# Cross-attention, Fourier mixing and FFN on one core: the Fourier stage on folded data, attention with block-diagonal state, u kept on chip, the row scale behind the second matmul

## The chip, the cores and the metric

One core of one Trainium2 chip. The metric is device time in microseconds. The engines of a core take their instructions in the order of their own list and wait on semaphores: PE (matrix multiply, with PEld loading its weights), DVE (vector), ACT (scalar functions), POOL and SP, both of which also issue DMAs.

## The reference

Eight batches. Attention runs in both directions between x (8 heads, 512 rows, 64 wide) and a small state (32 rows a head); the results are joined to 544 rows of 512, mixed by the real part of a two-dimensional Fourier transform, normalised by row, and sent through an FFN of 512 to 2048 to 512.

```
scores = scale * np.matmul(x, state.transpose(0, 1, 3, 2))      # 512 x 32 per head
xread  = softmax(scores) @ state
sread  = softmax(scale * np.matmul(state, x.transpose(0, 1, 3, 2))) @ x
x      = heads side by side of [xread, sread]                     # 8 x 544 x 512
u      = x + np.real(fft(fft(x, axis=1), axis=2))
un     = (u - mean) / np.sqrt(var + 1e-06)                        # by row
out    = u + np.maximum(un @ w_ch1, 0.0) @ w_ch2
```

(softmax is written out in the reference, and the joining is shortened here.)

## The kernel before

First the tables of cosines and sines are computed (L21, on DVE and ACT: CN, SNneg for the columns, CM, SM for the rows), and both weights are loaded on POOL's queue (L100, L101). Then `fft_attention(b)` for the eight batches, then `ffn(t)` for 34 tiles of 128 rows. A scheduler turns this program into one list per engine, so that FFN tiles of early batches stand between the attention steps of later ones; what depends on what is enforced by semaphores, and pools of buffers (psA with tags qa and qb, psF with ph and po, all in PSUM) limit how far a stage runs ahead.

`fft_attention(b)` loads x and state (L112, L114) and takes two heads at a time (the loop at L126). For each pair: x is transposed (L131, xTp to xT), the scores of x against the state are one matmul per head and 128 rows, 32 columns wide (L138, psc); exp, row sums, and eight scalings on DVE (L148, a); eight transposes back (L152); xread by matmuls that fill half the partitions (L160). The other direction makes scores 32 x 512 (L168), exp (L172), scale (L174), transposes (L178), and then the result twice, once in each orientation: srp (L189) and srTp (L191) alternate, 64 and 32 columns each.

The Fourier stage multiplies the transposed rows by CN and SNneg (L206, L208, 288 of the 512 columns, the rest by mirroring at L213 and L214), and then by CM and SM over the five row chunks: for each of five tiles of output rows, ten matmuls of 512 columns (L222, L225, pMix). x itself is transposed back (L231) and added (L234, u). u is written to DRAM (L237); mean and variance (L240, L241), the square root on ACT (L243), the reciprocal, the scaled row un (L248), and its transpose (L252, unTp) go to unT_all on chip.

`ffn(t)` takes 128 rows: 64 matmuls of 128 columns (L268, ph_p), ReLU on ACT (L270, hT), 16 matmuls of 512 columns (L273, po); u is read back from DRAM (L276), added (L278, ot), and stored (L279).

## Time and profile before

| | us |
|---|---|
| median of 3 runs (lowest, highest) | 682.48 (681.53, 682.55) |
| the profiled execution: span from first to last instruction | 674.9 |
| PE busy / DVE busy / ACT busy | 598.5 / 319.3 / 273.3 |
| first matmul of attention (L117) waits for | 48.2 |
| last matmul of the FFN (L273) ends, last ot (L278) begins | 671.05 |

The profile follows one execution. For this execution it gives its span; the times of the runs are a little longer than the span, since they include what lies around it. Line numbers are those of the listing. In the lists of groups, "out<-in" names the tiles, then partitions x elements and type, the count, the busy time in us, the mean duration of one in ns, and behind the last bar the idle time ahead of the group and what ended it. In the chain and in the timeline the first two numbers are the start and the duration in us. A row of a stretch gives, after its bounds, the length, and then for PE, PEld, DVE, ACT and POOL the busy time and the count of instructions, then the granted clock, the share of DMA and GB/s. Matmuls are pipelined: the duration of one is longer than the step from its start to the next one's.

### The profile page before, as it was taken

To read this page: it belongs to the slowest core of one execution; us is meant where nothing else is said; L and a number is where in the kernel's file an instruction comes from. 1 tells how busy PE (TensorE), PEld (TensorE's weight loads), DVE (VectorE), ACT (ScalarE), POOL (GpSimd) and SP (SyncE) were. 2 spreads that over 40 slices of the span, in tenths; PEclk is the share of its full clock that TensorE was granted. 3 is DMA by queue.
4 is the path that set the end of the run, shared out by engine and by line. 5 is a ranking of instruction groups with operands and counts; after the bars stand their busy time and mean duration, and the time that the engine had idled before them with its cause. 6 is when DMAs were issued, how large, how long until landed. Compare 5 with 4: busy or idle time off the path is not lost. (4 is left out here: it accounts for less than half of the span.)

```text
span 674.9 us, 13333 instructions
## 1 busy us (share of the span) xinstructions
PE 598.5 (89%) x5648; PEld 376.1 (56%) x5648; DVE 319.3 (47%) x962; ACT 273.3 (40%) x601; POOL 39.3 (6%) x60
## 2 busy tenths in 40 slices
PE   0006689999999999999999999999999999999997
PEld 0003455665566746665566566655655566567775
DVE  8934334644554556445644654464436543611010
ACT  2212224633453436353634453355335533433322
POOL 2040010001000100010001100110000000000000
PEclk9999999999989999899999999998989898999999
DMA  7691052105211512151215211521102000222221
GB/s 138 112 59 8 0 34 83 65 17 50 79 52 34 50 63 66 35 48 49 80 35 35 80 51 32 50 84 33 32 9 90 33 33 1 98 63 82 77 64 48
DMA packets 52507, 36.24 MB, mean 54 GB/s; under 512 B 36832, under 2 KB 38880, under 8 KB 52448
## 3 DMA queue, kind: packets, MB, share of 16 engines
q0 software_dynamic: 37664, 8.65, 13.9%
q1 hardware_dynamic: 14784, 26.75, 11.8%
q8 instruction: 44, 0.72, 0.4%
q14 instruction: 15, 0.12, 0.1%
HBM read 26.21 MB, written 17.83 MB: 65 GB/s over the span
## 5 line engine op out<-in xcount | busy, mean ns | idle before, releaser
L268 PE MATMUL ph_p<-unT_all,w 128*128 128x128 bf16 x2176 | 148.5, 220 | 2.9 <-ACT hT L270 2.9
L273 PE MATMUL po<-w,hT 128*128 128x512 bf16 x544 | 144.8, 388 | 2.2 <-ACT hT L270 1.7
L268 PEld LDWEIGHTS <-w 128*128 128x128 bf16 x2176 | 126.5, 98 | 18.0 <-issue 6.1
L270 ACT ACTIVATE hT<-ph_p 128x512 bf16<-128x512 f32 x136 | 80.2, 598 | 87.6 <-PE ph_p L268 87.1
L273 PEld LDWEIGHTS <-hT 128*128 128x128 bf16 x544 | 46.4, 99 | 45.8 <-issue 4.5
L278 DVE TENSOR_TENSOR ot<-po,ut 128x512 f32<-128x512 f32 x34 | 23.4, 689 | 76.6 <-PE po L273 76.2
L133 DVE COPY xT<-xTp 64x1024 bf16<-64x1024 bf16 x32 | 21.8, 682 | 79.5 <-PE xTp L131 79.5
L189 PE MATMUL srp<-xin,a2T 128*32 128x64 bf16 x256 | 52.3, 207 | 1.5 <-DVE a2T L181 1.5
L191 PE MATMUL srTp<-a2T,xin 128*64 128x32 bf16 x256 | 52.4, 207 | 0.0
L222 PE MATMUL pMix<-A,CM 128*128 128x512 bf16 (+1 forms) x200 | 49.8, 379 | 2.1 <-DVE A L213 1.4
L225 PE MATMUL pMix<-Bm,SM 128*128 128x512 bf16 (+1 forms) x200 | 51.1, 379 | 0.0
L172 ACT ACTIVATE e<-p 32x512 f32<-32x512 f32 x64 | 37.3, 583 | 33.2 <-PE p L168 33.0
L234 DVE TENSOR_TENSOR u<-pMix,xbt 128x512 f32<-128x512 f32 x32 | 22.1, 691 | 55.7 <-ACT xbt L233 33.3
L117 PE MATMUL stTp<-ident,st 32*64 32x32 bf16 x64 | 3.5, 184 | 48.2 <-POOL xbS L124 48.2
L206 PE MATMUL pA<-CN,xbT 128*128 128x288 bf16 (+1 forms) x160 | 44.9, 311 | 0.0
L208 PE MATMUL pB<-SNneg,xbT 128*128 128x288 bf16 (+1 forms) x160 | 44.5, 310 | 0.0
L152 PE MATMUL aTp<-ident,a 128*32 128x128 bf16 x256 | 37.6, 234 | 7.1 <-DVE a L148 6.0
L210 DVE CAST A<-pA 128x288 bf16<-128x288 f32 (+1 forms) x40 | 18.2, 455 | 50.5 <-PE pA L206 50.5
L148 DVE TENSOR_SCALAR a<-e,ssum 128x32 bf16<-128x32 f32 x256 | 40.9, 234 | 0.9
L193 ACT CAST xbS<-srp 32x128 bf16<-32x128 f32 x32 | 8.2, 255 | 73.4 <-PE srp L189 73.4
L254 ACT COPY unT_all<-unTp 128x512 bf16<-128x512 bf16 (+1 forms) x40 | 20.4, 518 | 42.0 <-PE unTp L252 42.0
L152 PEld LDWEIGHTS <-a 128*32 128x32 bf16 x256 | 17.4, 98 | 34.1 <-DVE a L148 24.7
(81 smaller groups left out, 711.4 us busy)
## 6 DMA issues: line engine op xcount, KB each, us to landing
ut<-u_dram SPq DMA_DIRECT2D x34, 256.0 KB, 2.8
out_dram<-ot SPq DMA_DIRECT2D x34, 256.0 KB, 2.0
u_dram<-u SPq DMA_DIRECT2D x32, 256.0 KB, 2.0
w<-in_moe_w_ch_dram POOLq DMA_DIRECT2D x2, 2048.0 KB, 17.8
xin<-in_x_dram POOLq DMA_DIRECT2D x8, 512.0 KB, 7.0
u_dram<-u SPq DMA_DIRECT2D x8, 64.0 KB, 1.8
st<-in_state_dram POOLq DMA_DIRECT2D x8, 32.0 KB, 2.2
```

The costliest lines, as they stand in the source:

```text
L148: nc.vector.tensor_scalar_mul(a[:, hl, si, :], e[:, hl, si, :], ssum[:, hl, si, :])
L152: nc.tensor.transpose(aTp[:, hl, si, :], a[:, hl, si, :], ident)
L172: nc.scalar.activation(e2, p2, AF.Exp, scale=scale, accum_out=ssum2)
L189: nc.tensor.matmul(srp[:, hl, :], lhsT=a2T[:, hl, si, :], rhs=xhsi, start=(si == 0), stop=(si == SC - 1))
L191: nc.tensor.matmul(srTp[hl * 64:hl * 64 + 64, :], lhsT=xhsi, rhs=a2T[:, hl, si, :], start=(si == 0), stop=(si == SC - 1))
L206: nc.tensor.matmul(pA[:m_sz, :], lhsT=xbT[:, c, sl], rhs=CN[:, c, :], start=(c == 0), stop=(c == DC - 1))
L208: nc.tensor.matmul(pB[:m_sz, :], lhsT=xbT[:, c, sl], rhs=SNneg[:, c, :], start=(c == 0), stop=(c == DC - 1))
L222: nc.tensor.matmul(pMix[:m_sz, :], lhsT=CM[:, c, msl], rhs=A[:, c, :], start=(c == 0), stop=False)
L225: nc.tensor.matmul(pMix[:m_sz, :], lhsT=SM[:, c, msl], rhs=Bm[:, c, :], start=False, stop=(c == MC - 1))
L268: nc.tensor.matmul(ph_p[:, mcl, :], lhsT=w1[:, kc, mc * 128:(mc + 1) * 128], rhs=unT[:, kc, :], start=(kc == 0), stop=(kc == DC - 1))
L270: nc.scalar.activation(hT[:, half * MCPH:(half + 1) * MCPH, :], ph_p, AF.Relu)
L273: nc.tensor.matmul(po, lhsT=hT[:, kc, :], rhs=w2[:, kc, :], start=(kc == 0), stop=(kc == FC - 1))
```

## The change

The real part of the transform is the same at (row s, column n) and at (row -s, column -n). The new kernel uses this twice. Each batch's rows are put down as XF (rows 1 to 256) and XR (the mirrored rows 543 to 288, with their columns mirrored); Sm is their sum, and XE and XO are its even and odd parts over the columns, 256 wide (XN holds the middle column). One product with the row tables (gep, gop, 288 output rows, tables CT, ST, CL, SL) and one with the column table T2 (yp) serves both a row and its mirror: U is yp + XF and yp + XR. The 32 rows left (0 and 257 to 287) of four batches are collected in XL and GL, and make one tile of 128 for the FFN (`front_low`).

Attention takes four heads at once. The state stands block-diagonally in stb (four heads of 32 rows on 128 partitions, with columns of ones, so that a matmul gives the row sums too). xT is 128 partitions high; exp is taken on 128 x 1024 (ET in one orientation, E in the other); xread comes out in the needed row order, forwards or reversed, and DVE divides by the sums when it moves it out of PSUM (L278). The state's reads come as srp (257 columns) and are put into XR by eight small operations (L295).

u stays in SBUF. Rows are centred but not scaled before the transposes (ub, L349); since ReLU passes a positive factor, the scale of the row is applied behind the second matmul (L405: po times rstd, plus u). rstd is a power of -0.5 on POOL (L203) in place of the square root on ACT. The FFN takes the 512 rows of a batch at once (ph of 512 columns), with one ReLU in four on DVE (L396). Mirrored rows come out in reversed order: they go to DRAM (r_dram, L412), and from there reversed to the output (L413). x is loaded in five pieces (L74), two batches ahead; the weights in six (L84, L87), on POOL's queue ahead of the tables' iotas. psQ has two buffers of two banks for all of a front's products, psF two each for ph and po.

The new program is `front(b)`, then `ffn` of the batch before it. The removed lines are those of the listing above; these are added (cut to the core):

```diff
+    r_dram = nc.dram_tensor("r_dram", (B, 2, 128, dm), F32, kind="Internal")
+    def load_x(b):
...
+        for ps, si, rows in (
+            (slice(0, 128), 0, xb[1:129]),
+            (slice(0, 128), 1, xb[129:257]),
+            (slice(0, 1), 2, xb[0:1]),
+            (slice(1, 128), 2, xb[257:384]),
+            (slice(0, 128), 3, xb[384:512]),
+        ):
+            nc.gpsimd.dma_start(out=t[ps, si, 1:513].rearrange("p (h d) -> p h d", d=D), in_=rows)
+    load_x(0)
+    for q in range(4):
+        nc.gpsimd.dma_start(out=w1[:, :, q * 512:(q + 1) * 512], in_=w1v[:, :, q * 512:(q + 1) * 512])
+    load_x(1)
+    for q in range(2):
+        nc.gpsimd.dma_start(out=w2[:, q * 8:(q + 1) * 8, :], in_=w2v[:, q * 8:(q + 1) * 8, :])
...
+                nc.vector.tensor_scalar(f[:, i, :], in0=lf, scalar1=pf[:, c:c + 1], scalar2=None, op0=ALU.mult)
+            nc.vector.tensor_scalar(q, in0=f, scalar1=1.0 / N, scalar2=float(1 << 23), op0=ALU.mult, op1=ALU.add)
+            nc.vector.tensor_scalar(q, in0=q, scalar1=float(1 << 23), scalar2=-float(N), op0=ALU.subtract, op1=ALU.mult)
+            nc.vector.tensor_add(f, f, q)
+            nc.vector.tensor_scalar(q, in0=f, scalar1=-1.0, scalar2=None, op0=ALU.mult)
+            nc.vector.tensor_max(q, q, f)
...
+    psQ = ctx.enter_context(tc.tile_pool(name="psQ", bufs=2, space=bass.MemoryType.PSUM))
+    psF = ctx.enter_context(tc.tile_pool(name="psF", bufs=2, space=bass.MemoryType.PSUM))
...
+    def stats_of(u, name):
+        st6 = wk.tile([128, 6], F32, name="st6", tag="st6", bufs=4)
+        nc.vector.bn_stats(st6, u)
+        mv = wk.tile([128, 2], F32, name="mv", tag="mv", bufs=6)
+        nc.vector.bn_aggr(mv, st6)
+        nc.gpsimd.tensor_tensor(rstd, mv[:, 1:2], epst, op=ALU.add)
+        nc.gpsimd.tensor_tensor(rstd, rstd, mhalf, op=ALU.pow)
+        return mv, rstd
...
+    def front(b):
...
+            nc.tensor.transpose(sTp[:, 0, pr * 128:(pr + 1) * 128], sb[:, g, 4 + 128 * hp:132 + 128 * hp], ident)
+        sT = wk.tile([128, 4, 128], BF16, name="sT", tag="sT")
+        nc.vector.tensor_copy(sT, sTp[:, 0, 0:512].rearrange("p (a b) -> p a b", b=128))
...
+            for si in range(4):
+                o = (pr % 2) * 512 + si * 128
+                nc.tensor.transpose(xTp[:, g, o:o + 128], xin[:, si, 1 + 128 * pr:129 + 128 * pr], ident)
+        nc.vector.tensor_copy(xT[:, 0:2, :], xTp[:, 0, :].rearrange("p (a b) -> p a b", b=S))
+        nc.scalar.copy(xT[:, 2:4, :], xTp[:, 1, :].rearrange("p (a b) -> p a b", b=S))
...
+        for g in range(2):
+            for lo, hi, src in ((0, NM, slice(0, NM)), (NM, S, slice(S - 1, NM - 1, -1))):
+                for hp in range(2):
+                    nc.tensor.matmul(eTp[:, g, lo:hi], lhsT=sT[:, 2 * g + hp, :], rhs=xT[:, 2 * g + hp, src],
+                                     start=(hp == 0), stop=(hp == 1))
+        ET = wk.tile([128, 2, S], BF16, name="ET", tag="ET")
+        nc.scalar.activation(ET, eTp, AF.Exp, scale=scale)
...
+        for si in range(4):
+            for pr in range(4):
+                hp = pr % 2
+                nc.tensor.matmul(
+                    esp[:, si // 2, o:o + 64].rearrange("p (h j) -> p h j", j=Ns),
+                    lhsT=xT[:, pr, si * 128:(si + 1) * 128],
+                    rhs=sT[:, pr, 64 * hp:64 * hp + 64].rearrange("p (h j) -> p h j", j=Ns)[:, :, ::-1],
+                    start=True, stop=True)
+        nc.scalar.activation(E.rearrange("p a b c -> p (a b c)"), esp.rearrange("p a b -> p (a b)"), AF.Exp, scale=scale)
...
+        for g in range(2):
+            for si in range(4):
+                nc.tensor.matmul(srp[:, g, 0:257], lhsT=E[:, si, g, :], rhs=xin[:, si, 257 * g:257 * g + 257],
+                                 start=(si == 0), stop=(si == 3))
+        rcs = wk.tile([128, 2], F32, name="rcs", tag="rcs")
+        nc.vector.reciprocal(rcs, srp.rearrange("p g c -> p (g c)")[:, 0:769:768])
...
+        def xread(c0, rev, name):
+            p = q2(name)
+            for half in range(2):
+                g = 1 - half if rev else half
+                rhs = sb[:, g, 259::-1] if rev else sb[:, g, 4:264]
+                nc.tensor.matmul(p[:, half, 0:260], lhsT=ET[:, g, c0:c0 + 128], rhs=rhs, start=True, stop=True)
+            return p
...
+            rs = wk.tile([128, 2, 4], F32, name="rs", tag="rs", bufs=4)
+            nc.vector.reciprocal(rs[ps], p[ps, :, 256:260])
+            nc.vector.tensor_tensor(
+                o.rearrange("p (g h d) -> p g h d", g=2, d=D),
+                in0=p[ps, :, 0:256].rearrange("p g (h d) -> p g h d", d=D),
+                in1=rs[ps].unsqueeze(3).to_broadcast([n, 2, 4, D]),
+                op=ALU.mult,
...
+        for k in range(2):
+            p = xread(128 * k, False, "xfp")
+            normalise(p, XF[:, k, 0:512])
+            p = xread(256 + 128 * k, True, "xrp")
+            normalise(p, XR[:, k, 1:513])
+            if k == 0:
+                for g in range(2):
+                    for hh in range(4):
+                        c0 = 512 - (256 * g + 64 * hh)
+                        ph = slice(32 * hh, 32 * hh + 32)
+                        nc.vector.tensor_scalar(
+                            XR[0:32, 0, c0:c0 - 64:-1], in0=srp[ph, g, 1 - g + 64 * hh:65 - g + 64 * hh],
+                            scalar1=rcs[ph, g:g + 1], scalar2=None, op0=ALU.mult)
+        p = xread(256 - 32 * bq, False, "xlp")
+        normalise(p, XL[pq, 0:512], pq)
+        Sm = wk.tile([128, 2, 514], BF16, name="Sm", tag="Sm")
+        nc.vector.tensor_add(Sm, XF, XR)
+        nc.vector.tensor_add(XE[:, 0:2, :], Sm[:, :, 0:256], Sm[:, :, 512:256:-1])
+        nc.vector.tensor_sub(XO[:, 0:2, 1:256], Sm[:, :, 1:256], Sm[:, :, 511:256:-1])
+        nc.gpsimd.tensor_copy(XN[:, 0:2, 0:1], Sm[:, :, 256:257])
+        nc.vector.tensor_add(XE[pq, 2, :], XL[pq, 0:256], XL[pq, 512:256:-1])
+        nc.vector.tensor_sub(XO[pq, 2, 1:256], XL[pq, 1:256], XL[pq, 511:256:-1])
+        nc.gpsimd.tensor_copy(XN[pq, 2, 0:1], XL[pq, 256:257])
...
+        for j in range(2):
+            for c in range(3):
+                nc.tensor.matmul(gp[:, j, 0:NM], lhsT=XE[:, c, 128 * j:128 * j + 128], rhs=cos[c],
+                                 start=(c == 0), stop=(c == 2))
+        nc.scalar.copy(G[:, 0:2, :], gp[:, :, 0:NM])
...
+            for c in range(3):
+                nc.tensor.matmul(gp[:, j, 0:NM], lhsT=XO[:, c, 128 * j:128 * j + 128], rhs=sin[c],
+                                 start=(c == 0), stop=(j == 1 and c == 2))
+            if j == 0:
+                for c in range(3):
+                    nc.tensor.matmul(gp[:, 0, 0:NM], lhsT=XN[:, c, :], rhs=cos[c], start=False, stop=(c == 2))
+        nc.scalar.copy(G[:, 2:4, :], gp[:, :, 0:NM])
+        nc.gpsimd.tensor_copy(GLs[g4][:, :, 32 * bq:32 * bq + 32], G[:, :, 256:NM])
...
+        for k in range(2):
+            yp = q2("yp")
+            for c in range(4):
+                nc.tensor.matmul(yp[:, 0, :], lhsT=G[:, c, 128 * k:128 * k + 128], rhs=T2[:, c, :],
+                                 start=(c == 0), stop=(c == 3))
+            nc.vector.tensor_add(U[:, k, 0, 0:512], yp[:, 0, :], XF[:, k, 0:512])
+            nc.vector.tensor_add(U[:, k, 1, 1:512], yp[:, 0, 1:512], XR[:, k, 1:512])
+            nc.vector.tensor_add(U[:, k, 1, 512:513], yp[:, 0, 0:1], XR[:, k, 512:513])
+            for r in range(2):
+                u = U[:, k, r, r:r + 512]
+                mv, rstd = stats_of(u, "rstd")
+                rstds.append((k, r, rstd))
+                ub = wk.tile([128, 512], BF16, name="ub", tag="ub", bufs=4)
+                ud = u if r == 0 else U[:, k, 1, 512:0:-1]
+                nc.vector.tensor_scalar(ub, in0=ud, scalar1=mv[:, 0:1], scalar2=None, op0=ALU.subtract)
+                tp = q2("tp", BF16)
+                for j in range(DC):
+                    nc.tensor.transpose(tp[:, 0, 128 * j:128 * j + 128], ub[:, 128 * j:128 * j + 128], ident)
+                col = (2 * (1 - r) + k) * 128
+                nc.scalar.copy(unT[:, :, col:col + 128], tp[:, 0, 0:512].rearrange("p (a b) -> p a b", b=128))
...
+    def front_low(g4):
+        yp = q2("yp")
+        for c in range(4):
+            nc.tensor.matmul(yp[:, 0, :], lhsT=GLs[g4][:, c, :], rhs=T2[:, c, :], start=(c == 0), stop=(c == 3))
+        U = wk.tile([128, 512], F32, name="UL", tag="UL")
+        nc.vector.tensor_add(U, yp[:, 0, :], XLs[g4][:, 0:512])
...
+        hT = wk.tile([128, FC, 512], BF16, name="hT", tag="hT")
+        for f in range(FC):
+            ph = psF.tile([128, 512], F32, name="ph", tag="ph")
+            for c in range(DC):
+                nc.tensor.matmul(ph[:, :n], lhsT=w1[:, c, f * 128:(f + 1) * 128], rhs=unT[:, c, :],
+                                 start=(c == 0), stop=(c == DC - 1))
+            if f % 4 == 3:
+                nc.vector.tensor_scalar_max(hT[:, f, :n], ph[:, :n], 0.0)
+            else:
+                nc.scalar.activation(hT[:, f, :n], ph[:, :n], AF.Relu)
+        for i, (u, rstd, dst) in enumerate(tiles):
+            po = psF.tile([128, dm], F32, name="po", tag="po")
+            for f in range(FC):
+                nc.tensor.matmul(po, lhsT=hT[:, f, i * 128:(i + 1) * 128], rhs=w2[:, f, :],
+                                 start=(f == 0), stop=(f == FC - 1))
+            ot = wk.tile([128, dm], F32, name="ot", tag="ot", bufs=3)
+            nc.vector.scalar_tensor_tensor(ot, in0=po, scalar=rstd, in1=u, op0=ALU.mult, op1=ALU.add)
...
+                nc.sync.dma_start(out=r_dram[b, k], in_=ot)
+                nc.sync.dma_start(
+                    out=out[b, top:top - 128:-1, :].rearrange("r (c n) -> c r n", c=2),
+                    in_=r_dram[b, k].rearrange("r (c n) -> c r n", c=2))
...
+    ready = [front(0)]
+    for b in range(B):
+        if b + 1 < B:
+            if b + 2 < B:
+                load_x(b + 2) if b + 2 >= 2 else None
+            ready.append(front(b + 1))
+        ffn(*ready[b])
+        if b % 4 == 3:
+            ffn(*front_low(b // 4))
```

Where the instructions now stand. On ACT before, in the midst of the span, ReLUs of the FFN (hT) stand between the steps of one head pair's attention (e is an exp, xbT and xbS are copies of attention's results):

```order
L162 CAST xbT<-xrTp 128x512
L193 CAST xbS<-srp 32x128
L194 CAST xbT<-srTp 128x32
L141 ACTIVATE e<-psc 128x256
L270 ACTIVATE hT<-ph_p 128x512
L172 ACTIVATE e_1189,ssum_1190<-p_1187 32x512
L172 ACTIVATE e_1196,ssum_1197<-p_1194 32x512
L270 ACTIVATE hT<-ph_p 128x512
L162 CAST xbT<-xrTp 128x512
L270 ACTIVATE hT<-ph_p 128x512
```

On ACT of the new kernel, fronts 1 to 4 have eight ReLUs between E and the two copies of G; front 1 is this:

```order
L230 COPY xT<-xTp 128x1024
L398 ACTIVATE hT<-ph 128x512
L240 ACTIVATE ET<-eTp 128x1024
L254 ACTIVATE E<-esp 128x1024
L398 ACTIVATE hT<-ph 128x512 x8
L319 CAST G<-gep 128x576
L328 CAST G<-gop 128x576
L398 ACTIVATE hT<-ph 128x512 x3
L354 COPY unT<-tp 128x4x128 x4
```

and further on, behind the low tile's twelve ReLUs, fronts 5 and 6 are these:

```order
L230 COPY xT<-xTp 128x1024
L240 ACTIVATE ET<-eTp 128x1024
L254 ACTIVATE E<-esp 128x1024
L319 CAST G<-gep 128x576
L328 CAST G<-gop 128x576
L354 COPY unT<-tp 128x4x128 x4
L230 COPY xT<-xTp 128x1024
L240 ACTIVATE ET<-eTp 128x1024
L254 ACTIVATE E<-esp 128x1024
L319 CAST G<-gep 128x576
L328 CAST G<-gop 128x576
L398 ACTIVATE hT<-ph 128x512 x12
```

In fronts 5 and 6 no ReLU stands between xT and G: what FFN work there is comes behind.

On POOL before, at the program's start, ident and the iotas of the tables come first, and the loads of the weights and of x behind them:

```order
masks.py:197 MEMSET ident 128x128
L27 ISA
L27 IOTA l_i 128x288
masks.py:199 AFFINE_SELECT ident<-ident 128x128
L36 IOTA p_i 128x288
L27 IOTA l_i 128x544
L36 IOTA p_i 128x544
L100 DMA w_221<-in_moe_w_ch_dram 128x4x2048
L101 DMA w_222<-in_moe_w_ch_dram 128x16x512
L112 DMA xin<-in_x_dram 128x32x64
```

and in the new kernel:

```order
L84 DMA w_69<-in_moe_w_ch_dram 128x4x512
L74 DMA xin_60<-in_x_dram 128x8x64 x2
L74 DMA xin_60<-in_x_dram 1x8x64
L74 DMA xin_60<-in_x_dram 127x8x64
L74 DMA xin_60<-in_x_dram 128x8x64
L84 DMA w_69<-in_moe_w_ch_dram 128x4x512 x3
L74 DMA xin_61<-in_x_dram 128x8x64 x2
L74 DMA xin_61<-in_x_dram 1x8x64
L74 DMA xin_61<-in_x_dram 127x8x64
L74 DMA xin_61<-in_x_dram 128x8x64
L87 DMA w_70<-in_moe_w_ch_dram 128x8x512 x2
masks.py:197 MEMSET ident 128x128
```

Here sixteen issues (x2 and x3 are repeated rows) stand ahead of ident, and the iotas follow it.

More of the change, by code (lines that the diff above doesn't have):

```diff
@@ L71 @@
     Ns = state.shape[2]
[L72 removed]
+    dm = H * D
     Stot = S + Ns
@@ new lines @@
+    stf = singles.tile([128, B, 2, D], F32, name="stf")
+    nc.sync.dma_start(
+        out=stf.rearrange("p b g d -> p (b g) d"),
+        in_=state.rearrange("b (g hh) j d -> (hh j) (b g) d", hh=4),
+    )
+    xin_bufs = []
+    for i in range(2):
+        t = singles.tile([128, 4, 514], BF16, name=f"xin{i}")
+        xin_bufs.append(t)
+    def load_x(b):
+        t = xin_bufs[b % 2]
+        xb = x[b].rearrange("h s d -> s h d")
+        for ps, si, rows in (
[6 more added lines that the diff above has]
+            nc.gpsimd.dma_start(out=t[ps, si, 1:513].rearrange("p (h d) -> p h d", d=D), in_=rows)
```

375 lines of the change are left out of this document (156 added, 219 removed).

## The prediction

> **What bounds the kernel now.** I read the page's first two parts, then three stretches of the span, then the chain that ended last and the waits.
>
> ```profile
> span 674.9 us, 13333 instructions
> PE 598.5 (89%) x5648; PEld 376.1 (56%) x5648; DVE 319.3 (47%) x962; ACT 273.3 (40%) x601; POOL 39.3 (6%) x60
> PE   0006689999999999999999999999999999999997
> 48.60:97.50 48.90, 34.93 (x257) 21.70 (x256) 19.43 (x70) 13.15 (x36) 2.78 (x4) 1.00 0.24 16
> 120.00:590.00 470.00, 461.39 (x4311) 283.69 (x4309) 242.14 (x760) 211.94 (x481) 22.38 (x31) 0.98 0.22 49
> 597.19:671.00 73.81, 73.81 (x816) 52.83 (x814) 6.92 (x10) 24.49 (x41) 0.00 (x0) 1.00 0.20 66
> PE stTp L117 <- POOL xbS L124: 48.2, 1, 48.2
> ```
>
> PE is the bound from 120 us on (461 of 470 us busy); the first 48.2 us it waits for the tables and the first load. Busy is not full speed, so I take the pitch (start to start) from rows in sequence: the chain's tail for the FFN, the timeline for the rest.
>
> ```profile
> 642.86 3.58 PE ph_p L268 x64
> 646.44 3.45 PE po L273 x16
> 671.05 0.69 DVE ot L278
> 300.60 0.29 PE L206 MATMUL pA<-CN,xbT 128*32 128x288 bf16 x1
> ...
> 301.21 0.29 PE L208 MATMUL pB<-SNneg,xbT 128*32 128x288 bf16 x1
> 329.69 0.20 PE L189 MATMUL srp<-xin,a2T 128*32 128x64 bf16 x1
> 329.82 0.20 PE L191 MATMUL srTp<-a2T,xin 128*64 128x32 bf16 x1
> 318.95 0.36 PE L138 MATMUL psc<-stT,xT 64*128 64x32 bf16 x8
> 319.24 0.23 PE L268 MATMUL ph_p<-unT_all,w 128*128 128x128 bf16 x1
> 93.43 0.45 PE L206 MATMUL pA<-CN,xbT 128*128 128x288 bf16 x1
> 93.67 0.45 PE L208 MATMUL pB<-SNneg,xbT 128*128 128x288 bf16 x1
> ```
>
> Pitches: 512 columns 3.45/16 = 0.216 us; 128 columns 3.58/64 = 0.056; 288 columns 0.61/5 = 0.122 (six starts, the middle ones left out); 32 columns 0.29/8 = 0.036. The pair L189/L191, of different tile shapes, costs 0.13 each for 64 and 32 columns: 512 of them take 67 us. Before 97 us everything runs at half pitch (0.24 for 288 columns), though the granted clock reads 1.00. One FFN tile takes 3.58 + 3.45 = 7.03 us; after 597.19 lie 73.81/7.03 = 10.5 tiles, so 23.5 tiles (165 us) lie between 48 and 597, and the other 384 us are attention and Fourier: **48 us a batch**.
>
> **The change, part by part.** *PE work.* A front (L206 of the new kernel: attention, folded Fourier, transposed un-scaled rows) has 36 transposes at 0.056, 16 score matmuls of 64 columns (between 0.036 and 0.056, I take 0.05), 4 of 288 and 4 of 224, 8 of 257, 10 of 260, 15 Fourier ones of 288 and 8 of 512; lengths between are interpolated (0.096, 0.109, 0.110). That is 2.0 + 0.8 + 0.5 + 0.4 + 0.9 + 1.1 + 1.8 + 1.7 = 9.2 us instead of 48. The FFN of a batch is 128 matmuls of 512 columns, 27.6 us; the two tiles of low rows cost 8.2 us each with their own transposes. Sum: 8 × 36.8 + 2 × 8.2 = **311 us**. The FFN alone hardly gains (34 × 7.03 = 239 against 235); the gain is in attention and Fourier.
>
> *The pace of one front.* Its steps depend on one another, mostly through DVE. Rows for that:
>
> ```profile
> L234 DVE TENSOR_TENSOR u<-pMix,xbt 128x512 f32<-128x512 f32 x32 | 22.1, 691 | 55.7 <-ACT xbt L233 33.3 <-issue 17.3 <-DMA ut<-u_dram 2.6
> L240 DVE BATCH_NORM_STATS2 stats<-u 128x6 f32<-128x512 f32 x32 | 22.0, 689 | 0.8
> L133 DVE COPY xT<-xTp 64x1024 bf16<-64x1024 bf16 x32 | 21.8, 682 | 79.5 <-PE xTp L131 79.5
> L148 DVE TENSOR_SCALAR a<-e,ssum 128x32 bf16<-128x32 f32 x256 | 40.9, 234 | 0.9
> L144 DVE RECIPROCAL ssum<-ssum 128x8 f32<-128x8 f32 x32 | 6.2, 195 | 0.8
> L241 DVE BATCH_NORM_AGGREGATE mv<-stats 128x2 f32<-128x6 f32 x32 | 5.6, 174 | 0.8
> L248 DVE TENSOR_SCALAR un<-u,neg_mu,rstd 128x512 bf16<-128x512 f32 x32 | 17.4, 545 | 1.0
> L46 DVE TENSOR_SCALAR q_f<-q_f 128x544 f32<-128x544 f32 x5 | 2.2, 435 | 0.0
> L48 DVE TENSOR_TENSOR f<-prod,q_f 128x544 f32<-128x544 f32 x5 | 3.6, 720 | 0.0
> L172 ACT ACTIVATE e<-p 32x512 f32<-32x512 f32 x64 | 37.3, 583 | 33.2 <-PE p L168 33.0
> L254 ACT COPY unT_all<-unTp 128x512 bf16<-128x512 bf16 x32 | 18.6, 582 | 40.9 <-PE unTp L252 40.9
> ```
>
> From the first transpose: transposes 1.1 and 0.2 until they have drained; ACT's half of xT, 1024 wide, 1.05 (between 0.58 and 1.17, twice the 512-wide row; nearer the double); eTp 1.1 with drain; exp ET 1.05, exp E 1.05; srp 1.1. Then DVE: five normalisations of 0.19 + 0.69, eight reads of srp at 0.2, Sm (1028 bf16: 0.69 if it ran at twice the f32 rate, 1.3 by L48's; I take 1.2), XE and XO 0.69 each, two of 0.43, a reciprocal: 9.6, and 1.2 for the two places where DVE waits for PE's next product. Then gop 1.0, G 0.65, the last two of yp 0.6. Sum **about 19.7 us from sTp to yp, in which PE has 7.5 us of work**; 12.2 are empty unless FFN matmuls stand between. From yp to the transposes of ub are 4.3 us more (U 1.54, statistics 1.38 + 0.35, ub 1.09), per half.
>
> DVE in all: 20 us a front and 5.5 for the batch's FFN; ACT 14. Against some 46 us a batch neither is the bound. What it removes of DMA (u out to DRAM and back) buys nothing: above, ph_p and po follow each other with nothing between.
>
> *Waits in PE's order.* I walked along the orders with these durations. In fronts 1 to 4 about 53 FFN matmuls (11.4 us) stand inside the 19.7, leaving some 4 us a front, at po behind E, at gep behind XE, and at the two tp: 16. Behind front 4, yp of the second half and the low tile wait 4.5 + 2.5, the low tile's ReLUs 1.6: 8.6. Front 5 has 8 FFN matmuls inside: 9.3, then 4.2 at its second half. Front 6 has none: 12.2. Front 7 has 8: 10.5. The rest (two tp, the second low tile, the last low ReLUs) 5. Sum **66 us**.
>
> *The start.* POOL issues 16 DMAs before it makes ident and the iotas.
>
> ```profile
> L112 POOL DMA_DIRECT2D xin<-in_x_dram x8 | 13.5, 1685 | 54.0 <-DVE CM L55 35.4 <-PE srTp L191 18.5
> L114 POOL DMA_DIRECT2D st<-in_state_dram x8 | 4.7, 584 | 227.4 <-PE xrTp L160 227.4
> L124 POOL MEMSET xbS<- 128x512 bf16 x8 | 4.2, 531 | 11.2 <-DVE u L236 11.2
> ```
>
> One issue costs 0.58 for 256 pieces and 1.69 for 4096, so 0.5 + 0.29 per thousand: 4 × 0.66 (w1), 2 × 3.7 (five for each x), 2 × 0.8 (w2) = 11.6 us. Ident, two memsets of 1152 (1.1 each) and the iotas take 5 more: 17.5 us. DVE then builds both tables, ten operations on 864 or 1024 columns and eight smaller at the rates of L46 and L48, 11.5 us: 29. Front 0 follows: 2.4 until xT is copied, 17.3 from there to yp, 4 because PE's links run at half pitch, as all of PE's work did before 97 us, 4.3 for each half, 0.6 for tp and 2.2 for the next front's transposes, which stand ahead of the first FFN matmul: 35 together, so **64 us** (bounds 58, if DVE's operations overlap, and 82, if xin is late, below).
>
> *The end.* The last ot 0.7, then eight stores on SP:
>
> ```profile
> 671.77 0.33 SPq L279 DMA_DIRECT2D out_dram<-ot  x1
> u_dram<-u SPq DMA_DIRECT2D x8, 64.0 KB, 1.8
> q1 hardware_dynamic: 14784, 26.75, 11.8%
> q0 software_dynamic: 37664, 8.65, 13.9%
> xin<-in_x_dram POOLq DMA_DIRECT2D x8, 512.0 KB, 7.0
> ```
>
> 8 × 0.33 + 1.8 + 0.7 = **5 us**. Four of them have 31 rows, which no row shows; q1 spent 0.118 × 16 × 674.9 / 26.75 = 48 engine-us a MB, so 4 × 64 KB all on one engine would last 12 us: 5 to 14. I take 5, from the 32-row store. Likewise the 127-row piece of x: spread, 7 us as xin's row; on one engine its 1016 packets last 28 (7.0 × 16/4096 each) to 41 us (q0's mean of 40 ns), and front 0 starts 5 to 18 us later. [...]
>
> The two stores and the reversed read through r_dram block SP for some 2 us each, beside 3.45 us of po; three ot buffers cover that.
>
> *Sum.* 64 + (311 − 10, done by then) + 66 + 5, + 3 while PE still runs at half pitch, + 3 for a granted clock of 0.98 in mixed work (row 120 to 590) = **442 us of span**. The span of before is 674.9, the median of its runs 682.48; the 7.6 between lie outside it: **450 us**.
>
> **Rivals.** *The waits vanish* (Sm, XE, XO fast, DVE's operations overlapping, fronts 5 to 7 covered): 0 to 40 us of 66 left, 384 to 424. For it: L148's 40.9/256 = 160 ns against 234 shows that DVE's operations overlap. Against: PE takes its instructions in the order given. 0.16.
>
> *PE falls back to half pitch.* From 48.6 to 97.5 us PE was 71% busy in small pieces and stayed at half; at 97.4, in a row of matmuls without a break, it changed, and never went back, with no wait above 1.5 us. In fronts 5 to 7 it is 38% busy, with gaps of 3 to 4 us. Falling back costs the doubled links of three chains (4 each) and about 2.5 each until it recovers: +20, 470. 0.14. [...]
>
> *The uneven DMAs go to one engine*: +5 to +18 and +9, 464 to 477. 0.13.
>
> *Slower than before*: PE never leaves half pitch, because no stretch is unbroken for long enough. Then 64 + 2 × 301 + about 20 + 5 + 7.6 = 699. Over 682 from a mean pitch of 1.8 times the full one. Against it are runs of 32 to 80 FFN matmuls (7 to 17 us) with nothing between; 0.015.
>
> **How the numbers follow.** Forecast 0.56, its own range 424 to 475; rivals as above, and 0.005 for no change. The range 412 to 492 leaves out the lower half of the first rival and the far ends of the others. A measurement tells 0.2% from no change: faster 0.98, within 0.005, slower 0.015.
>
> **What would show it.** Right: ph starts at 60 to 68 us; 0.216 us for 512 columns in po; ACT's chain ET, E, G in fronts 5 to 7 about 15 us with PE mostly empty; PE busy for about 75% of the span. Wrong: a steady PE without gaps in fronts 5 to 7, a first ph after 75, or 0.43 for 512 columns after 100 us.

## The result, and the profile after

The changed kernel takes 664.14 us (median of 4 runs, 661.32 to 664.79) against 682.0 of before: a ratio of 0.973 (0.970 to 0.976). The forecast was 450 us, its range 412 to 492. The direction came out, the size didn't: nine tenths of the expected gain is missing. The profiled execution took 664.54 us, with a span of 661.0.

The page of the kernel after, first parts, queues and groups:

```profile
span 661.0 us, 5124 instructions
...
PE 359.5 (54%) x1973; PEld 181.7 (27%) x2008; DVE 205.1 (31%) x470; ACT 130.2 (20%) x217; POOL 133.2 (20%) x170
...
PE   0000104138349907960990767237599949989970
...
PEclk9999997557859956995895788558589979999995
...
q0 software_dynamic: 159584, 8.88, 23.9%
...
L74 POOL DMA_DIRECT2D xin<-in_x_dram x40 | 79.4, 1993 | 247.2 <-issue 181.1
...
L327 PE MATMUL gop<-CT,XN 128*128 128x288 bf16 x16 | 5.3, 438 | 118.4 <-POOL XN L306 118.4
```

PE's work did shrink: 359.5 us busy in place of 598.5, much of it at half pitch (the mean granted clock is 0.829). But PE is busy for only 54% of the span: it has regular notches (the slices of 0 to 4 from the twelfth on), and the granted clock falls with them (down to 5 in the row PEclk). Before, PE was full from 120 us on, and behind the first 48.2 us it never waited for POOL (6% busy). Now POOL's busiest group is L74, the load of x, with 181.1 us of idle time ahead of it that the profile puts down to "issue", that is, to nothing else in the trace. And q0, the queue of POOL's loads, moves 159,584 packets where the kernel before moved 37,664, for about the same bytes (8.88 MB and 8.65).

The waits of the kernel after (us in total, times, the longest):

```profile
POOL xin L74 <- issue: 181.1, 16, 23.8
...
PE gop L327 <- POOL XN L306: 118.4, 6, 21.1
...
PE sTp L219 <- POOL ident masks.py:199: 79.4, 1, 79.4
```

PE waits for POOL seven times: once 79.4 us for ident, in the place of the 48.2 of before, and in six fronts about 20 us for XN, a copy that itself takes 0.2 us. POOL's timeline at the program's start and in front 1 shows what XN and ident stand behind (start, duration, group, and in brackets the idle time ahead):

```profile
2.20 2.32 POOL L74 DMA_DIRECT2D xin<-in_x_dram  x3
13.01 6.69 POOL L74 DMA_DIRECT2D xin<-in_x_dram  x1 [8.50 <-issue]
35.88 0.90 POOL L74 DMA_DIRECT2D xin<-in_x_dram  x1 [16.18 <-issue]
...
165.99 6.68 POOL L74 DMA_DIRECT2D xin<-in_x_dram  x1 [3.64 <-issue]
189.28 0.91 POOL L74 DMA_DIRECT2D xin<-in_x_dram  x1 [16.61 <-issue]
190.20 0.20 POOL L306 COPY XN<-Sm 128x2 bf16<-128x2 bf16 x1
```

The fourth issue of a load is the piece of 127 rows. It takes 6.7 us where three others together take 2.3, POOL stands still ahead of it, and behind it POOL does nothing for 16 us; only then come the fifth piece and XN. On PE, the first ph (behind front 0) starts at 153.29, and in front 1 gop waits for just that XN:

```profile
153.29 1.91 PE L393 MATMUL ph<-unT,w 128*128 128x512 bf16 x4
...
190.46 0.66 PE L327 MATMUL gop<-CT,XN 128*128 128x288 bf16 x2 [19.25 <-POOL XN L306]
190.91 0.45 PE L327 MATMUL gop<-CL,XN 128*128 128x288 bf16 x1
191.15 0.69 PE L323 MATMUL gop<-ST,XO 128*128 128x288 bf16 x2
...
635.72 5.77 PE L402 MATMUL po<-w,hT 128*128 128x512 bf16 x26
```

Behind the stall the starts lie 0.24 us apart for 288 columns (190.91 to 191.15): PE is back at half pitch, and so it is behind each of the six stalls. The view of the DMA issues (count, KB each, us to landing) sets the pieces side by side:

```profile
xin<-in_x_dram POOLq DMA_DIRECT2D x24, 128.0 KB, 4.3
...
xin<-in_x_dram POOLq DMA_DIRECT2D x8, 127.0 KB, 23.0
```

One row fewer, and the landing takes 23.0 us in place of 4.3. The packets set the piece apart too: a full piece has 128 x 8 runs of 64 numbers, 1024 packets. With 128 rows in place of the 127 (the first experiment below) q0 has 37,728 packets; the 121,856 more of this kernel are 15,232 a load, so the piece makes 16,256, which is 127 x 8 x 16. The expectations below take this for runs cut into sixteenths. The bytes say otherwise: 8.88 MB against 8.40 there, so that the further packets carry 4 bytes each, on top of the data. The sizes in the trace agree: 32,768 packets of 128 bytes, the whole runs of eight batches (64 numbers of 2 bytes), and 122,720 of 4 bytes, where the version with 128 rows has 800. Each run of the piece brings 15 packets of 4 bytes with it; what they are for, the trace does not say.

At the end the stores of SP reach far beyond PE, whose last po ends at 641.49 (the row above):

```profile
637.68 12.23 SPq L408 DMA_DIRECT2D out_dram<-ot  x10
```

The span ends 19.5 us behind PE, 11 us behind the last of these issues.

### The profile page after: what moved, and what is told of

The parts are those of the page before. It is cut to its first block, busy times and chain, and to the rows that moved or that the text cites. A ratio compares the mean times of both kernels' runs of the same rounds, so it can differ in the third digit from the quotient of the medians.

```text
span 661.0 us, 5124 instructions
## 1 busy us (share of the span) xinstructions
PE 359.5 (54%) x1973; PEld 181.7 (27%) x2008; DVE 205.1 (31%) x470; ACT 130.2 (20%) x217; POOL 133.2 (20%) x170
## 3 DMA queue, kind: packets, MB, share of 16 engines
q0 software_dynamic: 159584, 8.88, 23.9%
## 4 chain that ended last, share of the span: by engine, by line
PE 40%; issue 35%; POOL 13%; DVE 7%; ACT 2%; POOLq 0%; DVEq 0%; ACTq 0%
PE po L402 17%; PE ph L393 13%; POOL xin L74 10%; PE yp L338 3%; PE tp L352 1%; PE gop L323 1%; PE gop L327 1%; DVE XR L295 1%; DVE st L198 1%; PE eTp L237 1%; PE srp L260 1%; PE xTp L228 1%; ACT E L254 1%; DVE U L340 1%; DVE XF L278 1%
## 5 line engine op out<-in xcount | busy, mean ns | idle before, releaser
L74 POOL DMA_DIRECT2D xin<-in_x_dram x40 | 79.4, 1993 | 247.2 <-issue 181.1
L393 PE MATMUL ph<-unT,w 128*128 128x512 bf16 x496 | 125.9, 392 | 2.2 <-ACT hT L398 0.7
L402 PE MATMUL po<-w,hT 128*128 128x512 bf16 x532 | 121.8, 382 | 3.9 <-DVE ot L405 3.0
L398 ACT ACTIVATE hT<-ph 128x512 bf16<-128x512 f32 (+1 forms) x120 | 63.2, 535 | 111.7 <-PE ph L393 90.4
L393 PEld LDWEIGHTS <-w 128*128 128x128 bf16 x640 | 60.5, 102 | 61.9 <-issue 15.2
L327 PE MATMUL gop<-CT,XN 128*128 128x288 bf16 x16 | 5.3, 438 | 118.4 <-POOL XN L306 118.4
L396 DVE TENSOR_SCALAR hT<-ph 128x512 bf16<-128x512 f32 (+1 forms) x40 | 24.2, 604 | 132.6 <-PE ph L393 125.9
L219 PE MATMUL sTp<-ident,stb 128*128 128x128 bf16 x32 | 3.7, 250 | 79.9 <-POOL ident masks.py:199 79.4
L405 DVE SCALAR_TENSOR_TENSOR ot<-po,rstd,U 128x512 f32<-128x512 f32 x32 | 23.2, 746 | 38.9 <-PE po L402 38.8
L338 PE MATMUL yp<-T,G 128*128 128x512 bf16 x57 | 21.9, 485 | 2.4 <-ACT unT L354 1.1
L237 PE MATMUL eTp<-xT,sT 128*128 128x288 bf16 (+1 forms) x64 | 11.5, 310 | 20.7 <-DVE xT L229 20.4
L203 POOL TENSOR_TENSOR rstd<-rstd,mhalf 128x1 f32<-128x1 f32 x34 | 21.3, 626 | 2.7
L198 DVE BATCH_NORM_STATS2 st<-U 128x6 f32<-128x512 f32 x32 | 20.4, 681 | 0.0
```

The lines of the kernel that those rows point to most:

```text
L74: nc.gpsimd.dma_start(out=t[ps, si, 1:513].rearrange("p (h d) -> p h d", d=D), in_=rows)
L198: nc.vector.bn_stats(st6, u)
L203: nc.gpsimd.tensor_tensor(rstd, rstd, mhalf, op=ALU.pow)
L237: nc.tensor.matmul(eTp[:, g, lo:hi], lhsT=sT[:, 2 * g + hp, :], rhs=xT[:, 2 * g + hp, src], start=(hp == 0), stop=(hp == 1))
L338: nc.tensor.matmul(yp[:, 0, :], lhsT=G[:, c, 128 * k:128 * k + 128], rhs=T2[:, c, :], start=(c == 0), stop=(c == 3))
L393: nc.tensor.matmul(ph[:, :n], lhsT=w1[:, c, f * 128:(f + 1) * 128], rhs=unT[:, c, :], start=(c == 0), stop=(c == DC - 1))
```

## The experiments

Two theories stood at the outset. The first: the 127-row piece alone holds POOL, and what is queued behind it there holds PE. The rival: the five-piece load as such, or the amount of POOL work in a front, is too much. The kernel before ran beside each: 676.8 to 686.5 us beside the first four, 682.4 beside the next two, 676.8 to 684.2 beside the last four.

**Another division of the rows.** Five pieces as well, but 128 rows first and then row 0 over its first row:

```diff
-            (slice(0, 1), 2, xb[0:1]),
-            (slice(1, 128), 2, xb[257:384]),
+            (slice(0, 128), 2, xb[256:384]),
+            (slice(0, 1), 2, xb[0:1]),
```

> The third piece of x has 128 rows (256 to 383, on partitions 0 to 127) in place of 127, and row 0 is then put over partition 0; nothing else differs. Theory A (the 127-row piece is cut into very small packets, 16256 a load, which fill POOL's DMA queue; POOL stands still some 23 us at each load, and ident, the iotas and the copies XN stand behind it): PE's first matmul moves from 79 to about 17 us, the wait of gop for XN falls from 118 us to under 5, q0's packets from 160 thousand to about 37 thousand, and the span from 661 to 450 to 480. Theory B (XN only covers other waits of the fronts and the half clock, which then come out): the start gains its 60 us, the rest stays, about 600. Theory C (it is the odd destination address of x in SBUF that cuts the packets): packets and time stay, 655 to 665.

484.12 us, ratio 0.710 (0.698 to 0.722). The span, 481.4, lies just above the first theory's 450 to 480. PE no longer waits for XN; but its first matmul waits 31.8 us and not 17, since POOL first waits 15.7 us for earlier loads of x to land. And with the 127 rows as 112 and 15, which needs one more issue (lines from here on are one higher):

```diff
-            (slice(1, 128), 2, xb[257:384]),
+            (slice(1, 113), 2, xb[257:369]),
+            (slice(113, 128), 2, xb[369:384]),
```

> The 127 rows are loaded as 112 and 15. Theory A, in the form that the row count decides (no even share over 16 engines): the 112 rows issue in 0.8 us like 128; of the 15 rows either each run is cut, at most 1920 packets, or not, and POOL stands still under 4 us a load; span within 15 us of x128's. Rival (what matters is that the piece begins at partition 1 and not at 0): the 112-row piece stands still about as long as the 127-row one, 620 to 660.

479.87 us, ratio 0.704 (0.691 to 0.717). The queues and issues of this version, then POOL's timeline:

```profile
q0 software_dynamic: 37856, 8.39, 26.0%
...
xin<-in_x_dram POOLq DMA_DIRECT2D x8, 112.0 KB, 5.4
...
xin<-in_x_dram POOLq DMA_DIRECT2D x8, 15.0 KB, 4.7
```

```profile
2.21 4.64 POOL L75 DMA_DIRECT2D xin<-in_x_dram  x6
...
25.66 0.30 POOL masks.py:199 TENSOR_SCALAR_AFFINE_SELECT ident<-ident 128x128 bf16<-128x128 bf16 x1
```

Six issues now take 4.64 us without a break, the packets are back at the number of before, and PE no longer waits for XN. Both versions drop some 180 us, with as many pieces or one more: it is the piece, not the five-fold load. And the 112 rows start at partition 1 and at the same column as the 127 did, so the place of the piece is not it either.

**The copies of XN off POOL.** The loads stay as changed; the two copies go to DVE:

```diff
-        nc.gpsimd.tensor_copy(XN[:, 0:2, 0:1], Sm[:, :, 256:257])
+        nc.vector.tensor_copy(XN[:, 0:2, 0:1], Sm[:, :, 256:257])
...
-        nc.gpsimd.tensor_copy(XN[pq, 2, 0:1], XL[pq, 256:257])
+        nc.vector.tensor_copy(XN[pq, 2, 0:1], XL[pq, 256:257])
```

> The two copies XN go to DVE; the loads stay as they are. Theory A: POOL stands still as before, at the start too (PE's first matmul stays at 79 us), but gop no longer waits: 118 us less, and some more as PE's clock stays up: span 525 to 560. Theory B: the waits come out elsewhere (rstd, also on POOL, holds ot, and so po and PE): 620 to 660.

546.99 us, ratio 0.802 (0.784 to 0.820). A wait and a group of it:

```profile
PE sTp L219 <- POOL ident masks.py:199: 79.6, 1, 79.6
```

```profile
L74 POOL DMA_DIRECT2D xin<-in_x_dram x40 | 79.5, 1994 | 224.8 <-issue 75.2 <-PE srp L260 55.3 <-PE ph L393 25.5
```

POOL stands almost as long ahead of L74 as it did (224.8 us against 247.2; part of it now bears the name of whatever ended on PE at that moment), and ident is as late as ever. But what a front still has behind it on POOL, GL and rstd, is needed late, and 117 us are gone: the 118.4 of gop's waits, almost to the number. That it comes so close is luck. The two runs lie 6.7 us apart, and gep now waits 12.1 us for what DVE does around the new copies: five of the eight (15.9 us in all) start while POOL issues the piece, last 1.5 to 5.0 us, and end with that issue, where the other three last 0.15 to 0.17. What offsets these 12 us was not taken apart. This separates the stall (POOL's) from its price (PE's, through the order on POOL).

**The same loads in the kernel before.** If the piece is the cause, it must hurt the old kernel too:

```diff
-        nc.gpsimd.dma_start(out=xin, in_=x[b].rearrange("h (sc p) d -> p h sc d", p=128))
+        xr = x[b].rearrange("h (sc p) d -> p h sc d", p=128)
+        for ps, si in ((slice(0, 128), 0), (slice(0, 128), 1), (slice(0, 1), 2), (slice(1, 128), 2), (slice(0, 128), 3)):
+            nc.gpsimd.dma_start(out=xin[ps, :, si, :], in_=xr[ps, :, si, :])
```

> The kernel before, with x loaded in the five pieces of the new kernel (128, 128, 1, 127, 128 rows) and nothing else changed. Theory A (a stuck POOL costs only what stands behind it): the two loads at the start hold up the memsets that the first matmul waits for, 48 to about 85 us or more, and later loads are covered, since POOL is 6% busy: 715 to 750. Rival (each load costs its 23 us, wherever it stands): 830 or more. If the form of the load costs nothing: 682.

750.94 us, 1.101 (1.082 to 1.120) times the kernel before, just above the expected range. POOL's timeline:

```profile
45.99 6.68 POOL L114 DMA_DIRECT2D xin<-in_x_dram  x1 [2.87 <-issue]
68.47 0.90 POOL L114 DMA_DIRECT2D xin<-in_x_dram  x1 [15.80 <-issue]
```

The same 6.68 and the same 16 us, with other tiles and other neighbours. The stall belongs to the transfer. Its price here is paid in two ways. The first matmul waits 72.4 us in place of 48.2, for the state, whose load stands behind the piece on POOL. And later loads are not covered, though the expectation has them so: pMix waits 33.2 us in all for A, where it waited 1.4 before. DVE's copy of A takes 0.50 us; in three batches it starts while POOL issues the piece, takes 6.5 us and ends 0.3 us behind that issue, and in three others the operation on Bm ahead of it is held in the same way (4.2 to 5.6 us in place of 0.5).

**What about 127 rows, and what POOL waits for.** First 126 rows and one row:

```diff
-            (slice(1, 128), 2, xb[257:384]),
+            (slice(1, 127), 2, xb[257:383]),
+            (slice(127, 128), 2, xb[383:384]),
```

> The piece of 127 rows is loaded as 126 rows and one row; all else as in the changed kernel. Theory (127 has no divisor from 2 to 16, 126 has 14, and it is that which has the runs of 64 elements cut up): q0 carries about 38 thousand packets in place of 159,584, POOL never stands still for 16 us behind an issue, and the time is that of the versions with 128 and with 112 + 15 rows, 476 to 492 us. Rival (any number of rows above 16 that is not a multiple of 16 is cut up): q0 stays near 155 thousand packets, POOL stands still as before, 645 to 680 us.

477.91 us (one run), and of its queues and issues:

```profile
q0 software_dynamic: 39008, 8.40, 26.1%
...
xin<-in_x_dram POOLq DMA_DIRECT2D x8, 126.0 KB, 5.7
```

The theory's numbers: 126 rows do not bring the many packets, though 126 is no multiple of 16. Then the 127 rows in two transfers of four heads:

```diff
...
+            if ps == slice(1, 128):
+                nc.gpsimd.dma_start(out=d[:, 0:4, :], in_=rows[:, 0:4, :])
+                nc.gpsimd.dma_start(out=d[:, 4:8, :], in_=rows[:, 4:8, :])
...
```

> The piece of 127 rows is loaded in two transfers of four heads each, 127 rows both; all else as in the changed kernel. Theory (the number of cut-up packets counts: POOL's queue holds only so many, and POOL stands until they have moved): q0 still about 159 thousand packets, each half's issue 3.3 us, and from the start of the first half's issue to the next issue behind the second about 23 us as now; the matmuls gop still wait some 18 to 20 us in six fronts; 650 to 675 us. Rival (one transfer that large is the trouble, and halves fit into the queue side by side): POOL goes on to its next instruction within 2 us of the second issue, no gop wait above 5 us, 485 to 540 us.

561.18 us (one run), between the two expectations, and both failed. POOL's timeline:

```profile
4.50 4.61 POOL L76 DMA_DIRECT2D xin<-in_x_dram  x1
13.09 4.56 POOL L77 DMA_DIRECT2D xin<-in_x_dram  x1 [3.98 <-issue]
17.90 0.91 POOL L79 DMA_DIRECT2D xin<-in_x_dram  x1 [0.24 <-issue]
```

q0 still has 159,712 packets, so the number of packets alone is not the price: the same packets hold POOL from 4.50 to 17.90, 13.4 us, where the whole piece held it from 4.52 to 35.88, 31.4 us; gop's waits fall from 118.4 to 50.4 us. The first half is issued at once, where the whole one waited 8.50 us; the second waits 4 us. So size counted more than in proportion here. With the whole piece, POOL's next issue starts about when the piece has landed (13.01 + 23.0, the median landing, is 36.0, and the next issue starts at 35.88); what POOL waits for there, and in the 8.50 us ahead of the piece, the trace does not say.

**What is left without the stall.** The version with 112 + 15 rows is the change as it was priced, and still 30 us over the forecast. Its windows (bounds, length, busy PE, PEld, DVE, ACT, POOL, clock, DMA, GB/s), then PE's timeline:

```profile
79.00:220.00 141.00, 135.76 (x812) 68.78 (x811) 79.90 (x192) 51.03 (x80) 33.80 (x64) 0.99 0.34 42
220.00:306.00 86.00, 58.93 (x371) 33.21 (x369) 40.99 (x101) 17.65 (x33) 12.07 (x28) 0.76 0.18 34
```

```profile
79.19 1.06 PE L394 MATMUL ph<-unT,w 128*128 128x512 bf16 x2
...
220.93 0.61 PE L353 MATMUL tp<-ident,ub 128*128 128x128 bf16 x8
...
226.31 1.04 PE L353 MATMUL tp<-ident,ub 128*128 128x128 bf16 x8 [3.30 <-DVE ub L350]
...
245.74 0.40 PE L272 MATMUL xrp<-stb,ET 128*128 128x260 bf16 x2 [1.03 <-DVE XF L279]
247.17 0.40 PE L272 MATMUL xfp<-stb,ET 128*128 128x260 bf16 x2 [1.03 <-DVE XR L279]
249.55 0.59 PE L272 MATMUL xrp<-stb,ET 128*128 128x260 bf16 x2 [1.98 <-DVE XR L296]
...
274.98 0.58 PE L220 MATMUL sTp<-ident,stb 128*128 128x128 bf16 x4 [0.25 <-ACT unT L355]
...
298.07 0.60 PE L339 MATMUL yp<-T,G 128*128 128x512 bf16 x2 [0.30 <-ACT G L329]
```

The first ph starts at 79.19 (64 was forecast), fronts 1 to 4 are nearly gapless, the stretch from the end of front 4 to front 6 has a clock of 0.76. Three edits of this version, one for each of start, end and fronts 5 to 7, and all together.

*Start:* the block of loads, from load_x(0) to w2, moves behind ident, the memsets of CL and SL, the iotas and the tables, and ahead of the memsets of XF to XN.

```diff
-    load_x(0)
-    w1 = singles.tile([128, DC, dff], BF16, name="w1")
...
+    load_x(0)
+    w1 = singles.tile([128, DC, dff], BF16, name="w1")
...
```

> x112, with ident, the constants and the iotas ahead of the loads on POOL, and the fixed buffers' memsets behind them. Theory (in the start PE waits for the tables, and DVE builds them at half its rate while POOL writes its memsets: 288-wide multiplications at 1.0 us that are 0.3 in the kernel before): the tables are done by about 20 us, the first eTp moves from 48 to 21 to 26 us, span 450 to 456. Rival (x and w1 arrive later and take the place of the tables; DVE is as slow beside POOL's issues): first eTp at 35 or later, span 463 to 476.

452.23 us, ratio 0.663 (0.659 to 0.667), 28 less than without it; the span of 449.0 lies 1 us below the expected 450 to 456. DVE's timeline while it builds the tables, first with the loads ahead, where POOL's memsets of XF to XO run beside it:

```profile
30.05 3.99 DVE L146 TENSOR_SCALAR f<-l,pf 128x288 f32<-128x288 f32 x4
...
36.97 1.30 DVE L147 TENSOR_SCALAR q<-f 128x1024 f32<-128x1024 f32 x1
...
42.69 0.68 DVE L150 TENSOR_SCALAR q<-f 128x1024 f32<-128x1024 f32 x1
```

and with the tables first, where POOL issues DMAs in that time:

```profile
6.35 1.61 DVE L135 TENSOR_SCALAR f<-l,pf 128x288 f32<-128x288 f32 x4
...
9.55 0.69 DVE L136 TENSOR_SCALAR q<-f 128x1024 f32<-128x1024 f32 x1
```

The edit takes two things away at once: POOL's issues ahead of ident, and the memsets beside DVE. The traces split them. DVE begins the tables at 4.48 us in place of 28.08, 23.6 sooner, and they take 15.5 us in place of 18.7, 3.2 less; the first eTp starts at 21.08 in place of 47.91. So most of the gain is the order on POOL.

*End:* the stores of 31 rows as 16 and 15.

```diff
-            dst.append((slice(32 * bq + 1, 32 * bq + 32), out[b, 257:288, :]))
+            dst.append((slice(32 * bq + 1, 32 * bq + 17), out[b, 257:273, :]))
+            dst.append((slice(32 * bq + 17, 32 * bq + 32), out[b, 273:288, :]))
```

> x112, and the four 31-row stores behind each low tile are made as 16 and 15 rows. Theory (a transfer of 31 rows goes to one engine, as the 12 us of the prediction's upper bound; 16 and 15 rows spread): the 19 us from the last matmul's end to the span's end fall to 6 to 8, span 463 to 465. Rival (it is the number of stores and their issue that lasts, and four more are added): 476 to 480.

474.8 us, ratio 0.696 (0.692 to 0.700): 5 less, where 15 were hoped for, and with intervals that overlap; neither expectation fits. The trace tells more. SP's timeline:

```profile
457.95 14.02 SPq L410 DMA_DIRECT2D out_dram<-ot  x14
```

The transfers now end 2.6 us behind the last issue (457.95 + 14.02 = 471.97, span 474.6) in place of 11, so 31 rows were a long transfer. The first two of the fourteen stores have 128 rows; the twelve small ones behind them are issued in 8.1 us (from 463.87), where eight took 6.4. From PE's end to the span's end it is 12.6 us in place of 19.4; PE itself ended 5.4 us later in this execution (461.97 against 456.6), which hides most of the 6.8 in the span.

*Fronts 5 to 7:* both low tiles behind the last batch, so that front 5 has a full FFN beside it.

```diff
-        if b % 4 == 3:
-            ffn(*front_low(b // 4))
+    for g4 in range(2):
+        ffn(*front_low(g4))
```

> x112, with both low tiles behind the last batch, in place of one in the middle. By the order front 5 then has eight ReLUs inside, as fronts 1 to 4 have; fronts 6 and 7 have none, as before. Theory (a front without FFN work inside costs PE some 12 us of waits and then half clock, some 15 together, and the low tile in the middle 8): span 455 to 462. Rival (the waits move to other places): 472 to 480.

474.2 us, ratio 0.695 (0.692 to 0.698), 6 less (intervals that overlap again): the rival's range. PE's last row, then SP's:

```profile
447.55 2.10 PE L403 MATMUL po<-w,hT 128*128 128x512 bf16 x9
```

```profile
438.44 22.53 SPq L409 DMA_DIRECT2D out_dram<-ot  x18
```

PE is done at 449.7, 7 us sooner than the 456.6 without this edit, but the eighteen last stores on SP are issued until 460.97 and end the program, at 472.4: half of what PE won is lost there. The rest of the hoped-for gain went into waits and half pitch in front 6, as far as the windows show (0.86 from 220 to 290 us, 0.92 behind); that part was not taken apart further.

*All three:*

> The three edits together on x112. If each acts by itself: span 476 less 12, less 23, less 17, about 424, time 422 to 436. If they share waits (a shorter start or end that the others' waits swallow): 440 to 455.

435.13 us (433.02 to 435.93), ratio 0.638 (0.636 to 0.641): faster than both kernels. It lies in the range of the first expectation, but not by that expectation's terms: 12, 23 and 17 us were put in, 5.1, 27.6 and 5.7 came out of the single edits, 38 together, and the three at once gave 44.7. Why they give more together was not taken apart. What ends it:

```profile
409.56 18.71 SPq L410 DMA_DIRECT2D out_dram<-ot  x26
```

PE ends at 421.2, the span at 430.9: the small stores remain as the last chain.

## Why the prediction missed

**The sum of the changed kernel.** By the prediction's own terms, the profiled execution has: first ph at 153.3 where 64 was forecast (+89); from there to PE's end 488.2 where 373 was (442 - 64 - 5; +115); 19.5 behind PE where 5 was (+14.5); 3.5 outside the span in place of 7.6 (-4). That is all of the 214.9 between the terms (449.6) and 664.5. Of the 89, 62 are POOL's late ident (79.41 against 17.5) and 19 the first stall at gop; of the 115, 99.5 are the other five. What is left of both, 8 and 16 us, was not taken apart here.

**The step that failed** is the price of the 127-row piece. "The start" has "One issue costs 0.58 for 256 pieces and 1.69 for 4096, so 0.5 + 0.29 per thousand", by which the piece's 1016 runs are issued in 0.8 us; it took 6.69, and POOL stood still for 16 us behind it. "The end" counts "its 1016 packets", where there are 16,256, and lets "front 0" start "5 to 18 us later", once. The piece was seen, named as unknown, and bounded; but only its landing was priced, as data that front 0 waits for. It should have been priced as an instruction of POOL too: a transfer that by its own estimate may last 28 us or more may hold its issuer, and behind it on POOL stand ident once, and XN, on the path of gop, in every front that loads. The order of POOL's instructions was read at the start of the program and not within a front. The rival of the uneven DMAs had the right piece, and at most a tenth of its price (+5 to +18 where some 180 came).

That the piece and the 31-row stores each go to one engine, as the upper bounds in "The end" have it (28 to 41 us and 12 us), no run shows: the trace does not tell the engines apart. What the runs show is 15,240 packets of 4 bytes a load beside the piece's 1016 runs, and 23.0 us to landing; and the 31-row stores end 11 us behind their last issue, cut to 16 and 15 rows 2.6.

**The rest, read where the stall is gone** (112 + 15 rows, span 476.0):

- *The start*, 79.2 against 64. POOL had ident at 25.96 and the last iota at 28.8, not 17.5: with eighteen DMAs ahead it waits five times for earlier ones to land, 8.9 us in all. The tables took 18.7 us (28.08 to 46.80) and not 11.5. About 3 of these 7 us are POOL's memsets beside them, since the tables take 15.5 without (the *Start* edit), and 2 are ACT's last sines behind DVE's last product (44.71); the rest is DVE's work itself. Front 0 took 32.0 from the start of xT's copy to the first ph (47.17 to 79.19); 33.7 was forecast (35 less the 1.3 of the transposes).
- *PE's work and its waits*, 377.4 against 373: right by luck, since two errors cancel. PE waits 46 us and not 66, and is busy for 331 and not 307 (the work with its two terms of 3). Fronts 1 to 4 wait 5 us in all and not 16; about 4 of these 11 come from Sm at 0.70 and XE and XO at 0.42 us on DVE, not 1.2 and 0.69. The longer work is in the main half pitch, since the granted clock over this stretch is 0.92: front 6 took 23.5 us from sTp to the end of yp (274.98 to 298.51) and not 19.7, most of it at half pitch.
- *The rival "PE falls back to half pitch"* held, from the end of front 4 on. Eight transposes take 0.61 us at 220.93 and 1.04 at 226.31, behind a wait of 3.30. By 236 PE is at full pitch again; then two matmuls of 260 columns take 0.40 us up to 247.17 and 0.59 at 249.55, as at the program's start, with no wait above 1.98 in between. So in this trace PE fell back behind short waits too. The first three stretches at half pitch last some 10, 7 and 24 us (from 226, 250 and 274), where the rival put in 2.5 each, a figure that no run shows. And its evidence was misread: the kernel before did fall back after 97.4, six times for 3.4 us. The first time, from 196.5 to 199.9, its granted clock is 0.51 and three po take 1.49 us (198.16), where sixteen take 3.45 in the prediction's row; yet PE is busy for all of the 3.40 us. So there PE fell back without a wait; what sets it off was not tried.
- *The end*, 19.4 against 5: the lower bound was taken, the upper (14) was nearer. It is 1.7 us until the first small store, 6.4 for the eight of them (2.6 was forecast: a single one takes 0.23 to 0.33 us where nothing holds it, but some of them wait), and 11.3 until the last has landed (1.8, or 12 in the upper bound).
- *Outside the span*, 2.5 and not 7.6. The 7.6 compared the span of one execution with the median of others; a later run of before took 682.37 us with a span of 680.6, so the profiled execution had simply been a faster one.

15.2 + 4.4 + 14.4 - 5.1 are the 28.9 us between the terms' 449.6 and the 478.5 of this version's profiled run.

## What to carry to other kernels

Price a DMA twice, as data that lands (23.0 us for the piece here) and as an instruction of the engine that issues it (6.69, and 16 of standstill), and read what stands behind it there: POOL, 6% busy before and 20% after, set the pace here. Count the packets a transfer makes: one row fewer than 128 made 16,256 in place of 1024. When a change hits one stage with a long stall, first remove the stall with the smallest edit, then read the other terms; here all of them were off as well, in both directions.

## What the hardware showed that was not expected

- A load of 127 rows of 8 x 64 (f32 to bf16, on POOL's queue) moves 16,256 packets: its 1016 runs whole, 128 bytes each, and 15 packets of 4 bytes for each run. It takes 23.0 us to landing, with 6.69 us of issue and 16 us of standstill behind it. Loads of 128, 126, 112, 15 and 1 row of the same form show none of this (medians of 3.3 to 5.7 us to landing where the two halves of 127 rows aren't ahead of them). 126 has a divisor of 14, 127 none but 1; other such numbers were not tried. Whether the chip adds the packets, or what prepares the transfer for it, the runs do not show.
- An operation of DVE that starts while POOL issues this piece can last until the issue ends: the copy of A in the kernel before with the same loads took 6.49 us (202.99 to 209.48) in place of 0.50, POOL's issue going from 202.49 to 209.17. DVE's TENSOR_TENSORs in the changed kernel ran beside the same issue at their usual length (Sm 0.70 us at 167.60).
- DVE's TENSOR_SCALARs on f32 take up to 2.5 times as long beside POOL's memsets: four of 288 columns 3.99 us against 1.61, 1024 columns 1.30 against 0.69 (one of 1024, L148, took 0.70 there). Its TENSOR_TENSORs don't: 864 columns take 1.04 us with the memsets and without. What holds DVE there was not tried.
- The small last stores on SP, of 1 to 31 rows, follow each other at 0.5 to 1.0 us (eight in 6.4 us, twelve in 8.1, sixteen in 16.1, twenty-four in 12.2 with all three edits). A single issue that nothing holds takes 0.23 to 0.43, as the 0.33 of the store of 128 rows in the trace of before; the rest is waiting between them. What they wait for was not tried.
